# Local attention in front of two expert layers: filler products between half units taken out, weight loads and token preparation moved

## The chip, the cores and the metric

The kernel runs on one core of one Trainium2 chip. The metric is the device time of one execution in microseconds (us), as the median of several runs. A difference of less than about 0.2% can't be told from no change.

## The reference, cut to what matters

```python
# attention: batch 2, 8 heads, 768 positions, head_dim 64; chunks of 32 queries
for c in range(nc):
    k_full = concat([mem_k, k[l_start:r_end]])       # 8 memory keys, 16 left, 32 own, 8 right
    scores = scale * q_c @ k_full.T
    a = exp(scores - max(scores)); a = a / (sum(a) + 1e-9)
    out[chunk] = a @ v_full
x = out as 1536 tokens x 512
# layer 1: 4 experts (512 -> 1024 -> 512), summed with the tokens' probabilities p
for e in range(4):
    x1 += p[:, e] * (relu(x @ w1[e]) @ w2[e])
# layer 2: 512 -> 2048 -> 512, parametric relu
h = x1 @ w_in;  y = (max(h, 0) + alpha * min(h, 0)) @ w_out
```

## The kernel before

**Attention** is worked in 24 half units, numbered 0 to 23: a unit is 128 queries of one batch, a half unit four of its eight heads. The generator `half_unit` writes one out in five stages. `s`: 8 score products into a PSUM bank, then on VectorE (DVE) the row maximum `mx` and the subtraction into `pe_ring`. Then the exponential on ScalarE (ACT). `t`: four transposes of it on TensorE (PE) and their copy to `pt_ring` on ACT. `x`: 8 products with the values, then on DVE `dn`, `rd` and the normalised result `xs_t`. `xt`: two transposes of that and a copy to `acc` on ACT. After every fourth half unit a block of 128 token pairs is whole, and `prep_x` makes from it what the expert layers multiply: sums `st`, their rounded high part `xh` (casts on ACT) and the rest `xl`. For blocks 1, 2 and 5 (`FAST`) sums and rests are on DVE, for the others on POOL (GpSimd).

**The order of each engine** is fixed when the program is written out: a planner keeps a virtual clock `now`, to which each product adds a length (`T_S`, `T_X`, `T_T` for attention), and `att_poll` writes the next stage of a half unit once its latency (`LATE`, `LAT`) has passed on that clock. Up to four half units are live. Where no stage is due and nothing else may be written, `att_poll(force=True)` moves the clock on, and `fill` writes products of a zero tile `warm` (bank `wps`) for the time skipped, one per 0.11 us. 18 more stand at the very start.

**The expert layers** are products of 384 columns, in tiles of 384 token pairs: `gemm1` (banks a, b, c, d, then `g` and its high and low halves `gg`) and `gemm2` (banks `y`). The first tile needs blocks 0 to 2, the second blocks 3 to 5. So the program begins with attention alone, until half units 0 to 11 are done (here called **stretch A**); then comes `gemm1` of the first tile; then `gemm2` of the first tile, with the stages of the remaining half units written between its products; then, when those are used up, attention alone until half unit 23 is prepared; then `gemm1` of the second tile (from the first `gemm1` to here is **stretch B**). All that follows is products of the expert layers, with PE nearly full.

**Loads** are issued by the SP queue in program order. A half unit takes q (64x512 floats, 128 KB), k (64x672, 168 KB) and v (96x520, 195 KB). q and k have three buffers: those of half unit h+3 are issued after `s` of half unit h. Weights come as `raw` tiles of 512 KB (two for a pair of weight blocks) and are split into `wh` and `wl` by ACT and POOL. `gate` normalises the token probabilities on DVE, stores them (`p_dram`) and loads them back (`pb`), both on SP.

Of the kernel before, what the change touches and what calls it, by code (L numbers as in the profile page):

```python
# [30 lines left out]
NU = B * NBLK  # L31
# [36 lines left out]
def tile_kernel(ctx: ExitStack, tc: tile.TileContext, qk, mask, v, wa, wq, dpt, alpha, out):  # L68
    nc = tc.nc
    scale = 1.0 / float(D) ** 0.5  # L70
    pe_, dve, act, pool, sync = (Pinned(tc, e) for e in (nc.tensor, nc.vector, nc.scalar, nc.gpsimd, nc.sync))
# [7 lines left out]
    def bank(name):  # L79
        return ps.tile([P, 512], F32, tag="ps", name=name)  # L80
# [9 lines left out]
    nalpha = cp.tile([P, F2 // P], F32, name="nalpha")  # L90
# [4 lines left out]
    now = [0.0]  # L95

    def fill(n):

        if n > 0:
            wps = bank(f"wps{now[0]}")  # L100
            for _ in range(n):
                pe_.matmul(wps[:, :2 * P].rearrange("p (a n) -> p a n", n=P), warm, warm.unsqueeze(1).to_broadcast([P, 2, P]),
                           start=True, stop=True)
                now[0] += 0.11
# [5 lines left out]
    NI = NT // P  # L110
    p_dram = dp.tile([E, 2, NCOL], F32, name="p_dram")
    praw = cp.tile([P, E, NI], F32, name="praw")
# [82 lines left out]
    def load_v(hu):  # L195
        if hu >= 2 * NU:
            return
        u, half = divmod(hu, 2)
        dst = v_t[hu % RINGV // 2][:KEYS, hu % 2].rearrange("p w f -> p (w f)")
        sync.dma_start(dst, v[u, :, half])  # L200

    def half_unit(u, half):

        hu = 2 * u + half
        qv = q_t[hu % RING][:DQ].rearrange("p (h q) -> p h q", q=BLK)
        kv = k_t[hu % RING][:DQ].rearrange("p (h k) -> p h k", k=SPAN)
        vv = v_t[hu % RINGV // 2][:KEYS, hu % 2].rearrange("p w (h d) -> p w h d", d=D + 1)
        c, ab = divmod(u, 2)
        cols = slice(c * BLK, (c + 1) * BLK)
        hs = slice(2 * half, 2 * half + 2)  # L210
        nm = f"{u}_{half}"
        s_ps = bank(f"s{nm}")[:, :HH * KEYS].rearrange("p (h k) -> p h k", k=KEYS)
        for i in range(HH):
            for w in range(NW):
                r = slice(w * WIN, (w + 1) * WIN)
                mm(s_ps[r, i], qv[:, i, r], kv[:, i, w * STEP:w * STEP + KEYS], n=KEYS, took=T_S,
                   start=True, stop=True)
        load_half(hu + RING)
        mx = cp.tile([P, HH], F32, tag="mx", bufs=4, name=f"mx{nm}")
        dve.tensor_reduce(out=mx, in_=s_ps, axis=AX.X, op=ALU.max)  # L220
        pe = pe_ring[:, hu % 2]
        dve.tensor_tensor(
            out=pe, in0=s_ps, in1=mx.unsqueeze(2).to_broadcast([P, HH, KEYS]), op=ALU.subtract,
        )
        yield LATE
        act.activation(pe, pe, AF.Exp, scale=scale)
        yield LAT[0]
        t_ps = bank(f"t{nm}").rearrange("p (h q) -> p h q", q=BLK)
        for i in range(HH):
            pe_.transpose(t_ps[:KEYS, i], pe[:, i], ident)  # L230
            now[0] += T_T
        pt = pt_ring[:KEYS, hu % 2]
        act.copy(pt, t_ps[:KEYS])
        yield LAT[1]
        x_ps = bank(f"x{nm}")[:, :VW].rearrange("p (h d) -> p h d", d=D + 1)
        for i in range(HH):
            for w in range(NW):
                r = slice(w * WIN, (w + 1) * WIN)
                mm(x_ps[r, i], pt[:, i, r], vv[:, w, i], n=D + 1, took=T_X, start=True, stop=True)
        load_v(hu + RINGV)  # L240
        dn = cp.tile([P, HH, 1], F32, tag="dn", bufs=2, name=f"dn{nm}")
        dve.tensor_scalar_add(dn, x_ps[:, :, D:D + 1], 1e-9)
        rd = cp.tile([P, HH, 1], F32, tag="rd", bufs=2, name=f"rd{nm}")
        dve.reciprocal(rd, dn)
        xs = xs_t
        dve.tensor_tensor(out=xs, in0=x_ps[:, :, :D], in1=rd.to_broadcast([P, HH, D]), op=ALU.mult)
        yield LAT[2]
        xt_ps = bank(f"xt{nm}")[:, :2 * BLK].rearrange("p (c q) -> p c q", q=BLK)
        xf = xs.rearrange("p h d -> p (h d)")
        for z in range(2):  # L250
            pe_.transpose(xt_ps[:, z], xf[:, z * P:(z + 1) * P], ident)
            now[0] += T_T
        act.copy(acc[:, hs, ab, cols], xt_ps)
        if ab == 1 and half == 1:
            for _ in prep_x(c * BLK, BLK, c in FAST):
                yield 0.4

    att = {"next": 0, "start": 0.0, "done": 0, "over": set(), "live": [], "stage": [0] * (2 * NU + 1)}

    NEED = {0: 3, 2: 4}  # L260

# [6 lines left out]
    def att_poll(force=False):  # L268

        while True:  # L270
            due = [x for x in att["live"] if x[0] <= now[0] and clear(x[2])]
            room = att["next"] < 2 * NU and len(att["live"]) < LIVE and clear(att["next"])
            if due:
                x = due[0]
                try:
                    att["stage"][x[2]] += 1
                    lat = next(x[1])
                    x[0] = now[0] + lat
                except StopIteration:
                    att["live"].remove(x)  # L280
                    att["over"].add(x[2])
                    while att["done"] in att["over"]:
                        att["done"] += 1
            elif room and att["start"] <= now[0]:
                g = half_unit(*divmod(att["next"], 2))
                att["start"] = now[0] + (PACE0 if force else PACE)
                att["next"] += 1
                x = [0.0, g, att["next"] - 1]
                att["live"].append(x)
                x[0] = next(g) + now[0]  # L290
                att["stage"][x[2]] = 1
            elif force:
                times = [x[0] for x in att["live"] if clear(x[2])]
                if room:
                    times.append(att["start"])
                t = min(times)
                fill(int((t - now[0]) / 0.11))
                now[0] = max(now[0], t)
                continue
            else:  # L300
                return
            if force:
                return
# [6 lines left out]
    def load_raw(p, z):  # L310
        raw = bp.tile([P, 4, 256], F32, tag=f"raw{z}", name=f"raw{z}_{p}")
        src = wa[p] if p < NP1 else w2s[p - NP1]
        sync.dma_start(raw.rearrange("p a f -> p (a f)"), src[:, z * 1024:(z + 1) * 1024])
        raws[p, z] = raw
# [135 lines left out]
    pb_t = {}  # L450
# [186 lines left out]
    load_half(1)  # L637
    load_v(1)
    load_half(2)
    load_raw(0, 0)  # L640
    load_v(2)
    load_v(3)
    sync.dma_start(praw, dpt.rearrange("e (p i) -> p e i", i=NI))
    stream("w", weights())
    streams["w"][0] = PREP0
    acts = {}
    second = False
    for i, (what, k) in enumerate(order):
        p, c0, n = tiles[k]
        if what == 1:  # L650
            if p == 0:
                while att["done"] < 4 * -(-(c0 + n) // BLK):
                    att_poll(force=True)
                    prep_poll()
                    if att["next"] >= 4 and not second:
                        second = True
                        load_raw(0, 1)
                        nc.sync.dma_start(nalpha, alpha)
                    if att["done"] >= 4 and not pb_t:
                        gate()  # L660
                        dve.tensor_scalar_mul(nalpha, nalpha, -1.0)
                        load_pb(0, 0, FIRST[0][1])
            if k == k0:
                stream("c", convert())
                streams["c"][0] = now[0] + 20.0
            if k + 1 < len(tiles):
                p1, d0, m = tiles[k + 1]
                if p1 < NP1 and (2 * p1 * P // F1, d0, m) not in pb_t:
                    load_pb(2 * p1 * P // F1, d0, m)
            if p >= NP1 and f"x{c0}" in streams:  # L670
                prep_force(f"x{c0}", lambda: f"x{c0}" not in streams)
            hold[0] = p == 0
            acts[k] = gemm1(p, c0, n, k % 2 if p else 0, k == final[p])
        else:
            hold[0] = False
            change[0] = kx - 2 <= k <= kx + 1
            gemm2(p, c0, n, acts.pop(k), order[i - 1] == (1, k), k == final[p])
            if p == NP1 - 1:
                stream(f"x{c0}", transition(c0, n))
# [4 lines left out]

LAT = (1.0, 0.9, 1.3)
LATE = 1.5
T_S, T_X, T_T = 0.045, 0.036, 0.1
FAST = (1, 2, 5)
LIVE = 4
PACE = 2.3  # L690
PACE0 = 2.3
PREP0 = 6.0

DT = 1.1
DT_0 = 0.85
# [88 lines left out]
```

## Time and profile before

| | |
|---|---|
| median of 3 runs | 867.52 us (867.43 to 867.59) |
| profiled execution | 868.83 us, of it a span of 867.0 us |
| PE busy | 843.6 us (97%) |
| DVE busy | 607.1 us (70%) |
| POOL busy | 574.0 us (66%) |
| ACT busy | 336.4 us (39%) |
| first product of the first `gemm1` | at 62.62 us |
| first product of the second `gemm1` | at 106.62 us |

The span is what the trace covers; the profiled execution's own time is 1.83 us longer and lies 1.31 us above the median. A busy PE is not always useful: the filler products count as busy too, and matmuls overlap, so that two starts, not a duration, tell what one of them takes from the engine.

### The profile page before, as it was taken

To read this page: it belongs to the slowest core of one execution; us is meant where nothing else is said; L and a number is where in the kernel's file an instruction comes from. 1 tells how busy PE (TensorE), PEld (TensorE's weight loads), DVE (VectorE), ACT (ScalarE), POOL (GpSimd) and SP (SyncE) were. 2 spreads that over 40 slices of the span, in tenths; PEclk is the share of its full clock that TensorE was granted. 3 is DMA by queue.
4 is the path that set the end of the run, shared out by engine and by line. 5 is a ranking of instruction groups with operands and counts; after the bars stand their busy time and mean duration, and the time that the engine had idled before them with its cause. 6 is when DMAs were issued, how large, how long until landed. Compare 5 with 4: busy or idle time off the path is not lost.

```text
span 867.0 us, 14640 instructions
## 1 busy us (share of the span) xinstructions
PE 843.6 (97%) x5441; PEld 821.2 (95%) x5441; DVE 607.1 (70%) x1173; ACT 336.4 (39%) x738; POOL 574.0 (66%) x607
## 2 busy tenths in 40 slices
PE   7899999999999999999999999998799999999998
PEld 5788899999999999999999999997699999999998
DVE  2687676777767867678677677769867766776555
ACT  2465433323322323223232332324474645645442
POOL 2445447697766778669777697749567787774831
PEclk9999999999999999999999999999799999999999
DMA  9575211143122133212323213201011222121103
GB/s 186 150 192 140 60 49 49 38 128 116 37 85 85 63 113 107 63 60 87 108 68 104 85 37 103 72 9 50 24 49 62 86 86 97 54 70 37 62 1 146
DMA packets 28696, 69.76 MB, mean 80 GB/s; under 512 B 4664, under 2 KB 8888, under 8 KB 28624
## 3 DMA queue, kind: packets, MB, share of 16 engines
q1 hardware_dynamic: 28480, 68.76, 25.5%
q8 instruction: 43, 0.70, 0.3%
q14 instruction: 29, 0.24, 0.1%
q0 software_dynamic: 128, 0.04, 0.0%
q10 hardware_dynamic: 16, 0.02, 0.0%
HBM read 57.25 MB, written 11.56 MB: 79 GB/s over the span
## 4 chain that ended last, share of the span: by engine, by line
PE 88%; DVE 6%; ACT 2%; DMA 2%; POOL 1%; issue 1%; SPq 0%; DVEq 0%; POOLq 0%; ACTq 0%
PE y L62 45%; PE c L62 11%; PE a L62 11%; PE d L62 11%; PE b L62 5%; DVE st L62 2%; PE x L62 1%; PE s L62 1%; DVE xl L62 1%; PE t L62 1%; DMA k<-in_qk 1%; DVE g L62 1%; ACT xh L62 1%; DMA q<-in_qk 1%; DVE acc L62 1%
## 5 line engine op out<-in xcount | busy, mean ns | idle before, releaser
L62 PE MATMUL y<-gg,wh 128*128 128x384 f32 x1540 | 408.0, 341 | 8.4 <-POOL gg L62 4.8
L62 PEld LDWEIGHTS y<-gg,wh 128*128 128x128 f32 x1540 | 281.3, 190 | 11.7 <-POOL gg L62 6.4
L62 POOL TENSOR_TENSOR gg<-g,gg 128x384 fp32r<-128x384 f32 x192 | 198.6, 1043 | 107.7 <-ACT gg L62 96.2
L62 PE MATMUL y<-gg,wl 128*128 128x384 f32 (+1 forms) x770 | 260.8, 339 | 0.0
L62 DVE TENSOR_TENSOR acc<-y,acc 128x384 f32<-128x384 f32 x353 | 188.8, 551 | 67.3 <-PE y L62 66.1
L62 ACT CAST gg<-g 128x384 fp32r<-128x384 f32 x192 | 97.7, 511 | 169.8 <-DVE g L62 169.3
L62 POOL TENSOR_TENSOR wl<-raw,wh 128x256 fp32r<-128x256 f32 (+1 forms) x115 | 116.2, 1020 | 54.1 <-PE b L62 33.7
L62 PEld LDWEIGHTS y<-gg,wl 128*128 128x128 f32 x770 | 146.2, 190 | 0.2
L62 ACT COPY u<-a 128x384 f32<-128x384 f32 x48 | 23.0, 479 | 219.3 <-PE a L62 219.3
L62 POOL TENSOR_TENSOR wl<-s,wh 128x256 fp32r<-128x256 f32 x92 | 69.9, 767 | 16.4 <-ACT wh L62 16.2
L62 PE MATMUL c<-xh,wh 128*128 128x384 f32 x192 | 64.6, 336 | 2.0 <-DVE b L62 2.0
L62 PE MATMUL d<-xh,wh 128*128 128x384 f32 x192 | 64.4, 336 | 1.1 <-DVE t L62 1.1
L62 PE MATMUL a<-xh,wh 128*128 128x384 f32 x192 | 64.8, 338 | 0.3 <-ACT u L62 0.3
L62 PE MATMUL c<-xh,wl 128*128 128x384 f32 x192 | 64.5, 336 | 0.0
L62 PE MATMUL a<-xl,wh 128*128 128x384 f32 x192 | 64.4, 335 | 0.0
L62 PE MATMUL a<-xh,wl 128*128 128x384 f32 x192 | 64.3, 335 | 0.0
L62 PE MATMUL c<-xl,wh 128*128 128x384 f32 x192 | 64.3, 335 | 0.0
L62 PE MATMUL d<-xh,wl 128*128 128x384 f32 x192 | 64.2, 335 | 0.0
L62 PE MATMUL d<-xl,wh 128*128 128x384 f32 x192 | 64.2, 334 | 0.0
L62 DVE TENSOR_TENSOR u<-b,u 128x384 f32<-128x384 f32 x48 | 26.7, 557 | 51.4 <-PE b L62 46.9
L62 POOL TENSOR_TENSOR fl<-fl,fm 128x512 f32<-128x512 f32 x32 | 41.4, 1293 | 28.2 <-issue 19.0
L62 ACT CAST wh<-raw 128x256 fp32r<-128x256 f32 (+1 forms) x120 | 55.8, 488 | 0.9 <-PE a L62 0.6
(161 smaller groups left out, 1427.8 us busy)
## 6 DMA issues: line engine op xcount, KB each, us to landing
raw<-in_wa SPq DMA_DIRECT2D x32, 512.0 KB, 3.7
fr<-in_wq SPq DMA_DIRECT2D x32, 512.0 KB, 3.9
w2s<-fl SPq DMA_DIRECT2D x32, 256.0 KB, 2.3
raw<-w2s SPq DMA_DIRECT2D x16, 512.0 KB, 3.7
v<-in_v SPq DMA_DIRECT2D x24, 195.0 KB, 3.8
k<-in_qk SPq DMA_DIRECT2D x24, 168.0 KB, 3.5
q<-in_qk SPq DMA_DIRECT2D x24, 128.0 KB, 3.1
pb<-p_dram SPq DMA_DIRECT2D x8, 384.0 KB, 3.7
```

What stands on the lines that cost most here:

```text
L62: return self.tc.keep_in_program_order(f(*a, **kw))
```

## The change

The planner no longer writes filler products where it moves its clock on (the 18 at the start stay). Its lengths for attention's products are about doubled. The loads of the first weights, of the probabilities and of `alpha` are taken out of the head of the SP queue and are issued as later half units begin; `gate` waits for six half units done, not four; the preparation of weights starts at 12 on the planner's clock, not 6. `prep_x` of a block is not begun before the preparation of the block ahead of it is written out, and its steps on POOL are 1.0 apart, not 0.4.

```diff
         if ab == 1 and half == 1:
+            while att["x"] < c:
+                yield 0.2
             for _ in prep_x(c * BLK, BLK, c in FAST):
-                yield 0.4
+                yield 0.4 if c in FAST else 1.0
+            att["x"] = c + 1
...
-                t = min(times)
-                fill(int((t - now[0]) / 0.11))
-                now[0] = max(now[0], t)
+                now[0] = max(now[0], min(times))
...
     load_half(2)
-    load_raw(0, 0)
     load_v(2)
-    load_v(3)
-    sync.dma_start(praw, dpt.rearrange("e (p i) -> p e i", i=NI))
...
+    begun = [
+        (1, lambda: load_v(3)),
+        (1, lambda: load_raw(0, 0)),
+        (2, lambda: sync.dma_start(praw, dpt.rearrange("e (p i) -> p e i", i=NI))),
+        (6, lambda: sync.dma_start(nalpha, alpha)),
+        (7, lambda: load_raw(0, 1)),
+    ]
...
-                    if att["next"] >= 4 and not second:
-                        second = True
-                        load_raw(0, 1)
-                        nc.sync.dma_start(nalpha, alpha)
-                    if att["done"] >= 4 and not pb_t:
+                    while begun and att["next"] >= begun[0][0]:
+                        begun.pop(0)[1]()
+                    if att["done"] >= 6 and not pb_t:
...
-T_S, T_X, T_T = 0.045, 0.036, 0.1
+T_S, T_X, T_T = 0.095, 0.075, 0.105
-PREP0 = 6.0
+PREP0 = 12.0
```

The order on PE early in stretch A; a name such as `s1_0` is the bank of unit 1, half 0, which is half unit 2. Before:

```order
L62 MATMUL x0_0_200<-v0_110,pt_ring_113 64x65 x8
L62 LDWEIGHTS warm_74
L62 MATMUL wps4.447999999999997_215<-warm_74 128x256
L62 MATMUL s1_0_217<-k2_109,q2_106 64x96 x8
L62 LDWEIGHTS warm_74
L62 MATMUL wps4.959999999999999_231<-warm_74 128x256
L62 MATMUL t0_1_233<-ident_69,pe_ring_112 96x128 x4
L62 LDWEIGHTS warm_74
L62 MATMUL wps5.559999999999998_239<-warm_74 128x256
L62 MATMUL xt0_0_241<-ident_69,xs_t_114 128x128 x2
```

The same place in the changed program:

```order
L62 MATMUL x0_0_171<-v0_110,pt_ring_113 64x65 x8
L62 MATMUL s1_0_186<-k2_109,q2_106 64x96 x8
L62 MATMUL t0_1_200<-ident_69,pe_ring_112 96x128 x4
L62 MATMUL xt0_0_206<-ident_69,xs_t_114 128x128 x2
L62 MATMUL x0_1_210<-v0_110,pt_ring_113 64x65 x8
```

The stages follow each other in the same order and the `warm` products are gone. In the whole program 185 of them go, 133 in stretch A and 52 at the end of stretch B.

The order on SP, after the loads of the first two half units (`q2` is the third of the three buffers). Before:

```order
L62 DMA q2_106<-in_qk 64x512
L658 DMA nalpha_79<-in_alpha 128x16
L62 DMA k2_109<-in_qk 64x672
L62 DMA raw0_0_130<-in_wa 128x1024
L62 DMA v1_111<-in_v 96x520 x2
L62 DMA praw_100<-in_dpt 128x4x12
L62 DMA q0_104<-in_qk 64x512
L62 DMA k0_107<-in_qk 64x672
```

The same place in the changed program:

```order
L62 DMA q2_106<-in_qk 64x512
L62 DMA k2_109<-in_qk 64x672
L62 DMA v1_111<-in_v 96x520
L62 DMA q0_104<-in_qk 64x512
L62 DMA k0_107<-in_qk 64x672
L62 DMA v1_111<-in_v 96x520
L62 DMA raw0_0_146<-in_wa 128x1024
```

The 512 KB of weights, the `alpha` load and `praw` now stand behind q and k of half unit 3.

The order on ACT where block 0 is prepared: `xh<-st0` are the two casts that need POOL's sums, the `ACTIVATE` is an exponential, `pt_ring<-t3_1` the copy of half unit 7's transposes. Before:

```order
L62 CAST wh1_0_4_440<-s_0_265 128x256
L62 CAST xh_101<-st0_410 128x4x128
L62 COPY pt_ring_113<-t2_1_463 96x512
L62 COPY acc_103<-xt2_0_475 128x2x128
L62 CAST wh1_0_3_499<-s_0_265 128x256
L62 CAST xh_101<-st0_410 128x4x128
L62 ACTIVATE pe_ring_112<-pe_ring_112 128x384
```

The same work in the changed program:

```order
L62 CAST wh1_0_4_411<-s_0_287 128x256
L62 CAST xh_101<-st0_353 128x4x128
L62 COPY acc_103<-xt2_1_430 128x2x128
L62 CAST wh1_0_3_452<-s_0_287 128x256
L62 ACTIVATE pe_ring_112<-pe_ring_112 128x384
L62 COPY acc_103<-xt3_0_471 128x2x128
L62 CAST xh_101<-st0_353 128x4x128
L62 COPY pt_ring_113<-t3_1_476 96x512
```

The second cast stood ahead of half unit 6's exponential and one half unit behind the first; it now stands ahead of half unit 7's copy. From the first product of the second `gemm1` on, every engine has the same instructions in the same order in both programs.

## Rows read from the trace of the kernel before

**Rows 1.** Windows by stretch: length, busy us (instructions) by engine, clock, DMA share, GB/s.

```profile
0.00:62.62 62.62, 54.87 (x714) 43.38 (x714) 35.47 (x89) 27.87 (x63) 25.57 (x35) 0.95 0.75 177
62.62:70.80 8.18, 7.89 (x45) 7.27 (x43) 7.96 (x19) 2.94 (x7) 1.29 (x2) 1.00 0.61 169
70.80:97.20 26.40, 26.40 (x354) 22.16 (x352) 19.55 (x51) 15.11 (x34) 15.34 (x17) 1.00 0.38 104
97.20:106.62 9.42, 8.67 (x100) 7.48 (x99) 4.52 (x13) 4.36 (x10) 3.71 (x5) 1.00 0.19 60
```

**Rows 2.** Timeline of PE, first scores and half unit 3: start, length, idle before and releaser.

```profile
5.60 0.88 PE L62 MATMUL s<-k,q 68*64 68x96 f32 x16 [0.71 <-DMA k<-in_qk]
...
17.60 0.94 PE L62 MATMUL s<-k,q 68*64 68x96 f32 x16 [2.88 <-DMA k<-in_qk]
```

**Rows 3.** Window from the first loads to that wait's end.

```profile
2.00:17.60 15.60, 11.93 (x139) 9.15 (x136) 4.88 (x12) 3.66 (x8) 4.60 (x9) 1.00 1.04 210
```

**Rows 4.** Groups by form, 0 to 106.62 us: weight loads of all filler products.

```profile
L62 PEld LDWEIGHTS <-warm 128*128 128x128 bf16 x203 | 20.1, 105 | 6.3 <-DVE tiny L88 1.0 <-issue 0.2
```

**Rows 5.** Timeline of PE, one half unit's period in stretch A.

```profile
52.12 0.83 PE L62 MATMUL s<-k,q 68*64 68x96 f32 x16
52.88 0.64 PE L62 MATMUL t<-ident,pe_ring 128*96 128x128 f32 x4
53.36 0.60 PE L62 MATMUL ps28.832000000000058_828<-warm 128*128 128x256 bf16 x4
53.80 0.38 PE L62 MATMUL xt<-ident,xs_t 128*128 128x128 f32 x2
...
54.33 0.69 PE L62 MATMUL x<-v,pt_ring 96*64 96x65 f32 x16
...
55.27 0.88 PE L62 MATMUL s<-k,q 68*64 68x96 f32 x16
```

**Rows 6.** Timeline of DVE, the same period.

```profile
53.09 0.55 DVE L62 TENSOR_REDUCE mx<-s 128x4 f32<-128x384 f32 x1
53.74 0.56 DVE L62 TENSOR_TENSOR pe_ring<-s,mx 128x384 f32<-128x384 f32 x1
55.06 0.16 DVE L62 TENSOR_SCALAR dn<-x 128x4 f32<-128x4 f32 x1 [0.77 <-PE x L62]
...
55.47 0.42 DVE L62 TENSOR_TENSOR xs_t<-x,rd 128x256 f32<-128x256 f32 x1
```

**Rows 7.** Timeline of ACT, the same period.

```profile
53.62 0.58 ACT L62 COPY pt_ring<-t 96x512 f32<-96x512 f32 x1 [1.40 <-PE t L62]
...
54.49 0.53 ACT L62 ACTIVATE pe_ring<-pe_ring 128x384 f32<-128x384 f32 x1
```

**Rows 8.** Timeline of ACT, the second cast of block 0.

```profile
34.37 0.62 ACT L62 CAST xh<-st 128x512 fp32r<-128x512 f32 x1 [3.03 <-POOL st L62]
```

**Rows 9.** Windows, DVE alone: block 1's preparation (tile st); gate and alpha.

```profile
43.90:51.60 7.70, 3.71 (x6) 1.00 0.87 185
...
33.70:37.10 3.40, 3.17 (x8) 0.74 0.34 91
```

**Rows 10.** Timeline of PE, after that cast.

```profile
35.46 1.09 PE L62 MATMUL t<-ident,pe_ring 128*96 128x128 f32 x4 [2.43 <-ACT pe_ring L62]
...
37.97 1.03 PE L62 MATMUL x<-v,pt_ring 96*64 96x65 f32 x16
```

**Rows 11.** Windows as in rows 1, there and in the second layer's start.

```profile
35.00:40.00 5.00, 4.54 (x47) 3.73 (x48) 2.87 (x7) 1.97 (x5) 2.68 (x3) 0.66 0.13 29
606.00:612.00 6.00, 3.21 (x16) 2.25 (x15) 5.93 (x10) 4.76 (x10) 4.25 (x4) 1.00 0.00 0
612.00:614.00 2.00, 2.00 (x9) 2.00 (x8) 0.65 (x2) 1.29 (x3) 0.73 (x1) 0.55 0.00 0
```

**Rows 12.** Timeline of PE, end of stretch B: last transposes, first product of the second gemm1.

```profile
103.86 0.38 PE L62 MATMUL xt<-ident,xs_t 128*128 128x128 f32 x2
...
106.62 0.42 PE L62 MATMUL a<-xh,wh 128*128 128x384 f32 x1
```

More of the change, by code (lines that the diff above doesn't have):

```diff
@@ L254, in half_unit @@
         if ab == 1 and half == 1:
+            while att["x"] < c:
+                yield 0.2
             for _ in prep_x(c * BLK, BLK, c in FAST):
-                yield 0.4
-    att = {"next": 0, "start": 0.0, "done": 0, "over": set(), "live": [], "stage": [0] * (2 * NU + 1)}
+                yield 0.4 if c in FAST else 1.0
+            att["x"] = c + 1
+    att = {"next": 0, "start": 0.0, "done": 0, "over": set(), "live": [], "x": 0, "stage": [0] * (2 * NU + 1)}
     NEED = {0: 3, 2: 4}
@@ L646, in tile_kernel @@
     acts = {}
-    second = False
+    begun = [
[5 more added lines that the diff above has]
+    ]
     for i, (what, k) in enumerate(order):
```

## The prediction, written before the changed kernel ran

> **What bounds the kernel now.** I read the page first: PE is 97% busy, so only places where its work is not the expert layers' own, or where it waits, can give time. The window table by stretch shows where those are [rows 1]: stretch A, 62.62 us in which not one expert product runs; the first `gemm1`, 8.18 us; the interleaved part of stretch B, 26.40 us with PE busy throughout; and its end, 9.42 us of attention alone. In the busy time of A and of B's end the reader must see two things mixed, attention and filler. From 106.62 us on both programs have the same order on all engines, so I take the remaining 760 us as unchanged, and the prediction is when the second `gemm1` starts.
>
> How much the fillers weigh is read from the groups: 203 weight loads of `warm`, 18 of them at the very start, so 185 between half units [rows 4], 133 in A and 52 in B's end. One period of A in PE's timeline shows what one takes [rows 5]: scores start at 52.12, transposes at 52.88, four fillers run from 53.36 to 53.80 (0.11 us each), `xt` at 53.80, and the next scores start at 55.27. The period is 3.15 us; attention's own part is 0.76 (s) + 0.48 (t) + 0.22 (xt) + 0.62 (x) = 2.08 us, the rest is eight fillers and their gaps. So 185 fillers are 20 us of PE, but they are gained only if nothing else was being waited for beneath them. What else each half unit needs is on DVE [rows 6]: maximum and subtraction 53.09 to 54.30, 1.2 us, and `dn`, `rd`, `xs_t` 55.06 to 55.89, 0.83 us, so 2.03 us, nearly as much as PE's 2.08.
>
> **Stretch A, to half unit 6: the loads.** Half unit 3 waited for its k, 2.88 us, until 17.60 [rows 2], while the DMA share was 1.04 at 210 GB/s [rows 3]: that part was bound by loads, with 512 KB of weights ahead of that k. Now they stand behind it. To the k of half unit 6 the new list has 7 x 296 KB of q and k, 6 x 195 KB of v, 512 + 24 KB of others: 3778 KB, 3869 thousand bytes, 18.4 us at 210 GB/s. With the 2 us before the first bytes [rows 3] that is 20.4 us. But loads in flight share the rate: in before, half unit 3 needed 2568 thousand bytes in 15.6 us, 165 GB/s, by which it would be 25.4. I take 22 us, nearer to the fast end because less is in flight at once.
>
> **Half units 6 to 9: PE and one cast.** From s of 6 to s of 9 PE has 3 s, 3 t, 4 x, 4 xt: 2.28 + 1.44 + 2.48 + 0.88 = 7.1 us. Waits which fillers covered appear: from the end of t the copy takes until x may start (t ends near 53.4, copy 53.62 to 54.20 [rows 7], so 0.75 us), and where only `xt` stands between, 0.5 us is left, twice; an exponential may add 0.4 (scores end, then 1.2 us of DVE and 0.53 of ACT [rows 6, 7]). Sum 8.5. The second cast of block 0 waited 3.03 us for POOL's sums and ACT's queue waited with it [rows 8]; PE stood 2.43 us for it [rows 10]. In the new order it stands ahead of half unit 7's copy, and POOL's chain (eight operations after the block is whole) is as long as before while PE gets there sooner. Bounds: nothing, if the steps now 1.0 apart are slow enough, and 3.0 as before. I take 2.0, since the new order moves it back by one position only. So s of 9 starts at 22 + 8.5 + 2.0 = 32.5.
>
> **Half unit 9 to the first product: DVE.** From here DVE has more to do than PE: maximum and subtraction of 9 to 14, 6 x 1.2 = 7.2; `dn` to `xs_t` of 8 to 13, 6 x 0.83 = 5.0; gate and `alpha`, which filled 3.3 us of DVE [rows 9]; block 1's preparation, 3.7 [rows 9]; and four of six operations of block 2's, 2.2. Sum 21.4 us, from 33.4 (0.9 after the start of those scores) to 54.8; then `xt` of 13 and `x` of 14, 0.84. First product at 55.6 us in place of 62.62: **7.0 us** earlier. Gate also holds the SP queue (store, load back), so q and k of half units 13 and 14 come late; DVE is that far behind already, which hides it; without that cover I would price it as the one wait for a load in before, 2.88 us [rows 2].
>
> **The clock.** After PE stood 2.43 us the five microseconds from 35.00 have a mean clock of 0.66, that is 3.4 us at 1.2 GHz [rows 11], and t took 1.09 us there against 0.64, x 1.03 against 0.69 [rows 10, 5]. A fall does not need one long wait: from 606 to 612 PE was busy 3.21 of 6 us at full clock, and in the next two the mean was 0.55 [rows 11]. Without fillers A looks like that. The Trainium skill, "TensorE: Matmul & The Clock Gate", section "A second HAM failure mode: psum-queue depth-cycling", says that frequent short idle times between groups of matmuls make the clock swing between its two levels, and that throughput falls by the re-warming; rows 11 agree, and by it A would be the slow case below, 864 us. In my sum A costs nothing more, because the loads and then DVE set its pace and hide PE's doubled lengths; for the tail see next.
>
> **Stretch B.** `gemm1` 8.18 us as before: DVE was busy 7.96 of it, with the same work now. After it 8 s, 9 t, 9 x and 10 xt are left to do (in before 8, 10, 10 and 11), and the new order sets all but the last `xt` among the 48 y products or right behind them, where the old 26.40 us held 8 of each and left two t, two x and three xt to the bare end: 26.40 + 0.48 + 0.62 + 0.22, less gaps, 27.6. Then the bare end of half unit 23: 0.55 (copy before x), 1.05 (`dn` to `xs_t`, 0.83 and its start [rows 6]), and from the last `xt` to `gemm1` 106.62 - 103.86 = 2.76 [rows 12], a chain through ACT and POOL that fillers only accompanied. Sum 8.18 + 27.6 + 4.36 = 40.1 us against 44.0: **3.9 us**. PE stands for most of the last 4 us, so I expect `gemm1` to begin at 1.2 GHz; a spell of 3.4 us loses half of itself at most, 1.7; taken **1.5 us**, since in before this stretch was warm.
>
> **Sum.** 7.0 + 3.9 - 1.5 = 9.4 us. Against the execution's own 868.83 us that is 859.4; the median stands 1.3 us lower, so 858.1, rounded to **858 us**. The loads' upper bound (25.4) and the cast's (3.0) would add 4.4, the lower bounds take 3.6 off.
>
> **Rivals.**
> *Slow clock through A.* Without `warm` products PE drops to 1.2 GHz and stays there until `gemm1`. For: rows 11. Against: the loads and DVE have the pace anyway, and a PE that is twice as slow is also busier. Price: s about 1.4 (twice 0.76 less start cost, estimate), t 0.87, x 0.93, xt 0.4, so 3.6 us; 15 half units from 5.60 give 59.6. With `gemm1` begun cold (1.7) and B as above: gain 3.0 - 1.7 + 2.4 = 3.7, 864 us.
> *Slower than before.* The same, and the wait from t to x (0.55) is never covered: 4.15 us for each half unit, first product at 67.9, start of the second `gemm1` at 67.9 + 1.7 + 40.1 + 1.5 = 111.2, 4.6 us late: 872 us. It decides from 3.85 us for each half unit on (63.3 us for the first product, where B's gain is used up). Against: before's own period with fillers is 3.15, and its wait from t to x lay mostly beside the next s.
> *Loads alone.* If DVE's work packs into the load-bound part and the cast doesn't block, only the loads are left: 9093 KB to half unit 15's k and v of 14, 9311 thousand bytes, 44.3 us + 2 + the last products, first product at 48: gain 14.6 + 3.9 - 1.5 = 17.0, 850.5 us. Against: 35.47 us of DVE in A [rows 1] cannot begin before the first scores (6.5) and its gate and preparation come late in order.
> *No effect.* Every filler stood where something was awaited, so the waits stay: 866 to 869 us. Against: DVE 35.47 and PE's own 2.08 a period are both far below A's 62.62 us [rows 1].
>
> **Chances.** Forecast (853 to 861) 0.52; slow clock 0.20; loads alone (under 853) 0.15; no effect 0.05; slower 0.08. A measurement here can tell about 0.2%, 1.7 us. Faster by more: the forecast, loads alone, and most of the slow clock (0.17), 0.84; within: 0.03 of that and no effect, 0.08; slower 0.08. The range leaves one in ten out on each side: below, half of loads alone, 850; above, the slower case and a little of no effect, 866.
>
> **What would show it.** Half unit 3's scores start near 13 us with little wait for k; s of 6 near 22, of 9 near 32.5; DVE nearly gapless from there to the first `a` at 55 to 56 (a later one with PE's clock at 0.5 throughout is the slow clock; a DVE with gaps and a DMA share near 1 is loads alone); the second `gemm1` 9 to 11 us sooner than 106.62, its first 3 us at half clock; and from then on the old times, shifted. Wrong if the shift changes after the second `gemm1`, or if ACT's queue stands longer than 3 us behind the cast.

## The result: slower by 1.07%, and the profile after

The changed kernel takes 876.99 us (median of 4 executions, 876.87 to 877.41) beside 867.56 us of the kernel before: a ratio of 1.0107 [1.009, 1.0125]. The prediction had 858 us and a range that ended at 866, so it was wrong in sign, and the time lies above the range. The profiled execution took 877.41 us with a span of 875.6, 8.6 us more than before. Two slow executions among those of the experiments (1031.24 and 2113.6 us) are left out of all medians and ratios below.

On the page of after two lines of the 40 slices (21.9 us each) already show the place:

```profile
PE   8999989999999999999999999998699999999998
...
PEclk7557989999999999999999999999799999999999
```

PE is as busy in the first slices as anywhere, but its clock there is 0.7, 0.5, 0.5, 0.7. The windows of after, columns as in [rows 1], first by stretch and then more finely:

```profile
0.00:70.43 70.43, 64.96 (x602) 50.05 (x602) 37.27 (x95) 30.34 (x67) 24.46 (x35) 0.57 0.68 160
70.43:79.73 9.30, 9.30 (x45) 9.27 (x43) 7.05 (x16) 2.01 (x5) 1.71 (x2) 0.78 0.50 147
79.73:111.80 32.07, 28.87 (x378) 23.79 (x376) 22.31 (x60) 18.00 (x41) 17.76 (x19) 1.00 0.35 89
...
7.00:9.50 2.50, 1.46 (x20) 1.11 (x20) 1.29 (x3) 0.52 (x1) 0.00 (x0) 1.00 1.03 195
9.50:10.00 0.50, 0.00 (x0) 0.00 (x0) 0.47 (x2) 0.48 (x1) 0.00 (x0) 0.74 1.19 240
...
12.00:40.00 28.00, 26.96 (x254) 20.97 (x252) 12.47 (x33) 12.40 (x29) 12.10 (x15) 0.50 0.74 175
40.00:70.43 30.43, 29.24 (x276) 22.29 (x273) 21.86 (x54) 14.82 (x34) 9.46 (x11) 0.50 0.55 141
...
51.88:70.43 18.55, 18.54 (x171) 13.78 (x170) 11.68 (x27) 9.54 (x21) 4.85 (x5) 0.50 0.59 152
...
70.43:74.40 3.97, 3.97 (x14) 3.97 (x13) 2.25 (x5) 0.78 (x2) 0.70 (x1) 0.50 0.65 181
...
75.00:79.00 4.00, 4.00 (x25) 4.00 (x24) 3.82 (x9) 1.23 (x3) 1.01 (x1) 1.00 0.40 141
```

Stretch A ends at 70.43, not at 62.62 as in [rows 1] and not at the predicted 55.6. PE was busy 56.2 of the 58.4 us from 12.00 to 70.43 (96%), all of it at a clock of 0.50, the lower level of 1.2 GHz; DVE was busy 34.3 of them and the DMA share was 0.74 and 0.55. So PE had become the bound of A. From 51.88 on it didn't stand at all (18.54 of 18.55 us), and the clock stayed at 0.50 even so. PE's timeline of after shows where the clock fell, one period of A, and where the clock rose again (start, length, idle before and releaser):

```profile
8.03 0.88 PE L62 MATMUL s<-k,q 68*64 68x96 f32 x16 [1.45 <-DMA k<-in_qk]
8.84 0.64 PE L62 MATMUL t<-ident,pe_ring 128*96 128x128 f32 x4
10.15 1.14 PE L62 MATMUL x<-v,pt_ring 96*64 96x65 f32 x16 [0.67 <-ACT pt_ring L62]
...
51.88 1.55 PE L62 MATMUL s<-k,q 68*64 68x96 f32 x16
53.36 0.69 PE L62 MATMUL xt<-ident,xs_t 128*128 128x128 f32 x2
53.98 1.14 PE L62 MATMUL x<-v,pt_ring 96*64 96x65 f32 x16
55.05 1.09 PE L62 MATMUL t<-ident,pe_ring 128*96 128x128 f32 x4
56.07 1.55 PE L62 MATMUL s<-k,q 68*64 68x96 f32 x16
...
70.43 0.69 PE L62 MATMUL a<-xh,wh 128*128 128x384 f32 x1
...
74.12 0.53 PE L62 MATMUL b<-xh,wl 128*128 128x384 f32 x1
74.44 0.42 PE L62 MATMUL d<-xh,wh 128*128 128x384 f32 x1
74.69 0.34 PE L62 MATMUL d<-xl,wh 128*128 128x384 f32 x1
...
110.41 0.41 PE L62 MATMUL xt<-ident,xs_t 128*128 128x128 f32 x2 [1.03 <-DVE xs_t L62]
111.80 0.44 PE L62 MATMUL a<-xh,wh 128*128 128x384 f32 x1 [0.98 <-ACT xh L62]
113.20 0.69 PE L62 MATMUL a<-xl,wh 128*128 128x384 f32 x1 [0.96 <-POOL xl L62]
...
118.49 0.52 PE L62 MATMUL d<-xh,wl 128*128 128x384 f32 x1
118.81 0.42 PE L62 MATMUL a<-xh,wh 128*128 128x384 f32 x1
```

PE stood 1.45 us for a k and then 0.67 us for a copy, and the clock fell within the second of these waits (0.74 from 9.50 to 10.00, by which the fall is near 9.75); from then on x takes 1.14 us and s 1.55, beside 0.69 and 0.83 in [rows 5]. The period is read from start to start: from 51.88 to 56.07 it is 1.48 (s) + 0.62 (xt) + 1.07 (x) + 1.02 (t), together 4.19 us, with no wait in it. With eight fillers it was 3.15 [rows 5]. The k of half unit 3 is no longer waited for; that s starts at 15.18 instead of 17.60. The clock rises 4.0 us after the first expert product: the products stand 0.32 us apart until 74.44 and 0.17 to 0.18 from 74.69 on.

The account of the 8.6 us, from the starts of the two `gemm1`: stretch A +7.81 (70.43 against 62.62); the first `gemm1` +1.12 (9.30 against 8.18, begun at half clock); from there to the second -3.75 (32.07 against 35.82); and from its first product to the end of the span +3.42 (763.80 against 760.38). The last comes from the bare end: the second product waits for the rest `xl` until 113.20, and nearly all up to 118.81 stand 0.32 us apart. The 19th product starts 7.01 us after the first; in the kernel before, whose order is the same here, 3.23 us after its first, at 106.62 [rows 12]:

```profile
109.85 0.33 PE L62 MATMUL a<-xh,wh 128*128 128x384 f32 x1
```

### The profile page after: what moved, and what is told of

The parts are those of the page before. It is cut to its first block, busy times and chain, and to the rows that moved or that the text cites. A ratio compares the mean times of both kernels' runs of the same rounds, so it can differ in the third digit from the quotient of the medians.

```text
span 875.6 us, 14271 instructions
## 1 busy us (share of the span) xinstructions
PE 851.8 (97%) x5256; PEld 826.5 (94%) x5256; DVE 607.8 (69%) x1173; ACT 337.3 (39%) x738; POOL 573.5 (65%) x607
## 4 chain that ended last, share of the span: by engine, by line
PE 91%; DVE 5%; ACT 1%; issue 1%; DMA 1%; POOL 0%; SPq 0%; DVEq 0%; ACTq 0%
PE y L62 45%; PE a L62 11%; PE d L62 11%; PE c L62 11%; PE b L62 6%; PE s L62 3%; PE x L62 2%; PE t L62 2%; DVE st L62 2%; PE xt L62 1%; DVE xl L62 1%; DVE g L62 1%; DMA k<-in_qk 1%; DVE acc L62 1%; ACT xh L62 0%
```

## Experiments

Theory (**clock**): without fillers PE drops to 1.2 GHz in A, attention alone doesn't bring it back, and PE's doubled lengths set A's pace. Rival (**plan**): the moved loads, held preparation and new lengths make A longer, whatever the clock. Ratios are to the kernel before on the same chip, whose medians there were 866.4 to 867.0 us, with single executions from 863 to 873. With such a spread the intervals are up to 0.5% on either side, wider than the 0.2% that the prediction took as the least that can be told.

### Fillers and plan apart

*The new plan with its fillers:* the line that was removed stands again, with the new lengths (86 fillers in A, 45 at B's end).

```diff
-                now[0] = max(now[0], min(times))
+                t = min(times)
+                fill(int((t - now[0]) / 0.11))
+                now[0] = max(now[0], t)
```

> The changed program with its filler products back (the planner's clock, and so the order of everything else, stays as in the changed program; 86 fillers in stretch A, 45 at the end of stretch B). Theory clock: attention's own products do not hold PE at 2.4 GHz and the fillers do; then the loads and VectorE set A's pace as in the prediction, the first product comes near 55.6 us, the second gemm1 near 96 us, the median near 857 us. Rival order: the new order of loads and preparation is itself what costs; then the time stays at 872 to 877 us although the clock is full. Rival PE: in A fillers are on the path one for one, and the time goes back to 867.

*The old plan without fillers:* the kernel before with only the reverse of that edit.

> The kernel before with only its 185 fillers between half units taken out; the order of all else is as before. Theory clock: PE falls to 1.2 GHz near 10 us and stays there until the first gemm1, about 4.1 us for each half unit, first product at 68 to 71 us, median 874 to 879 us. Rival order: the loss comes from the moved loads and the held preparation, which are not here; then 855 to 867 us.

*Fillers at the end of B alone:* as the first, with `if att["done"] >= 12:` ahead of the `fill`.

> The changed program with fillers back only in forced waits after half unit 12, that is at the end of stretch B (45). Theory clock: A stays at 1.2 GHz (first product near 70 us as in the changed program); the second gemm1 begins at 2.4 GHz and gains the half of 5 us that it ran slow, so 873 to 875 us. Rival: the end of B waits for ACT and POOL alone and the fillers are worth nothing, 877 us.

Measured: 868.37 us, ratio 1.0032 [0.9996, 1.0067], for the new plan with fillers; 876.67, 1.0115 [1.0069, 1.0161], for the old plan without; 875.81, 1.0103 [1.0049, 1.0158], with fillers at B's end alone. So taking fillers out costs 1.15% (10 us) in the old plan and 1.0107 against 1.0032, or 0.75% (6.5 us), in the new, which the intervals don't tell apart; and the plan as a whole gains nothing with or without them. Of the forecasts the clock theory's for the old plan (874 to 879) was met; its 857 for the new plan with fillers was not, and that time lies nearest to the rival that puts the fillers on the path (867). The windows further down show what the theory had left out. PE's timeline of the old plan without fillers:

```profile
17.35 1.55 PE L62 MATMUL s<-k,q 68*64 68x96 f32 x16 [2.52 <-DMA k<-in_qk]
...
21.57 1.50 PE L62 MATMUL s<-k,q 68*64 68x96 f32 x16
...
25.73 1.49 PE L62 MATMUL s<-k,q 68*64 68x96 f32 x16
...
70.14 0.69 PE L62 MATMUL a<-xh,wh 128*128 128x384 f32 x1
```

The wait for k is the old one; the period of 4.16 us (a wait of 0.30 us ahead of x is part of it here) and the first product at 70.14 are close to those of after. The loads, moved or not, have no part in it. With fillers at B's end alone the first product comes at 71.21, cold; the second `gemm1` starts at full speed but at 114.58, 2.8 us later than in after. Its 19th product comes at 117.83 and not at 118.81: 1.0 us of the gain is left, less than the medians can tell. A window of that run and PE's timeline in the next:

```profile
20.00:40.00 20.00, 19.37 (x180) 14.59 (x176) 9.31 (x25) 9.08 (x21) 8.51 (x11) 1.00 0.54 152
```

```profile
48.75 1.54 PE L62 MATMUL s<-k,q 68*64 68x96 f32 x16
50.09 1.08 PE L62 MATMUL x<-v,pt_ring 96*64 96x65 f32 x16
```

The clock column reads 1.00 there and also from 40 to 70, but s takes 1.54 us, as at half clock in after. The other executions of this kernel show mean clocks of 0.955 at nearly the same spans (872.8 to 875.2 against 874.0), so the record of this one execution is wrong and the lengths decide.

In the new plan with its fillers the clock moves both ways:

```profile
15.00:20.00 5.00, 3.06 (x47) 2.39 (x44) 2.31 (x6) 2.28 (x5) 2.81 (x4) 1.00 1.07 207
20.00:25.00 5.00, 4.35 (x54) 3.52 (x56) 1.79 (x5) 1.38 (x3) 0.73 (x1) 0.74 0.69 151
25.00:30.00 5.00, 5.00 (x49) 3.71 (x47) 1.88 (x5) 2.64 (x7) 1.51 (x3) 0.58 0.76 217
30.00:40.00 10.00, 9.24 (x153) 7.53 (x151) 6.25 (x18) 6.37 (x16) 8.40 (x10) 1.00 0.55 158
40.00:45.00 5.00, 2.35 (x23) 1.54 (x19) 4.69 (x13) 2.51 (x7) 2.42 (x4) 0.79 0.15 34
45.00:50.00 5.00, 5.00 (x49) 3.85 (x49) 3.77 (x9) 2.20 (x6) 0.48 (x2) 0.53 0.86 220
50.00:60.00 10.00, 9.34 (x145) 7.22 (x140) 7.04 (x18) 6.30 (x15) 2.97 (x4) 1.00 0.94 213
```

```profile
36.96 0.83 PE L62 MATMUL s<-k,q 68*64 68x96 f32 x16
...
44.06 0.66 PE L62 MATMUL xt<-ident,xs_t 128*128 128x128 f32 x2 [2.50 <-DVE xs_t L62]
...
62.78 0.41 PE L62 MATMUL xt<-ident,xs_t 128*128 128x128 f32 x2 [1.42 <-DVE xs_t L62]
...
64.03 0.69 PE L62 MATMUL a<-xh,wh 128*128 128x384 f32 x1
```

The two falls shown here come after slices in which PE waited (busy 3.06 of 5 us, and 2.35 of 5), and each time the clock came back within A, which it never did in after. By the clock of these windows the two spells are 13.6 us at the lower level, an estimate of at most 6.8 us of lost work; the first product comes 8.4 us later than the forecast's 55.6. So fillers between the half units don't hold the clock through every wait. The long wait is no longer for a cast on ACT but for `xs_t`, which on DVE stands behind `gate` (39.06 to 42.31) and two sums of block 1.

### How many fillers

*One filler at most for each skip* (41 in all), *three at most* (96), and *half more* (206), each an edit of the `fill` line of the new plan:

```diff
+                fill(min(1, int((t - now[0]) / 0.11)))
...
+                fill(min(3, int((t - now[0]) / 0.11)))
...
+                t = max(now[0], t)
+                fill(int(1.5 * (t - now[0]) / 0.11))
+                now[0] = t
```

> The changed program with at most one filler in each forced wait (41 in all in place of 131). Theory clock, few are enough: the clock stays full in A and the time is near that of the program with all fillers, within 2 us. Theory clock, few are not enough: the clock falls near 10 us as in the changed program and the time is 874 to 879 us.

> The changed program with at most three fillers in each forced wait (96 of its 131). Theory clock: with more filler the fall comes later or is made good sooner than with one in each wait, so 867 to 871, between the program with all (868) and the one with at most one (871, runs from 866 to 876). Rival: any limit is as bad as none, 875 to 877.

> The changed program's order with one and a half times the fillers that its own forced waits give (206 in place of 131). Theory clock: the three falls of the clock in stretch A (near 22, 44 and 62 us) become fewer and the time is 862 to 866 although PE has 8 us more filler. Rival PE: the fillers are on the path and the time is 870 to 876.

Measured: 871.06 (865.67 to 875.85), ratio 1.0046 [1.0011, 1.0082]; 869.20 (864.34 to 872.17), 1.0029 [1.0004, 1.0055]; 871.72 (864.82 to 874.84), 1.005 [1.0023, 1.0077]. With at most one, single executions lie anywhere between after and the kernel before, and the profiled one (875.85) was cold, from 20 to 60 us at 0.50. The three differ from each other and from the full number by less than their intervals tell: few fillers recover part of the time in many executions, and more of them gain nothing further. The time with half more is the one that the rival with fillers on the path gave (870 to 876). Its profiled execution shows both sides: one fall of the clock in A fewer and the first product at 62.06 instead of 64.03, but 29 more fillers behind it and the second `gemm1` at 108.26 instead of 106.77.

*One burst:* after, with 40 fillers in a row when half unit 8 begins and none besides the first 18.

```diff
+                    if att["next"] == 8 and not burst:
+                        burst.append(now[0])
+                        fill(40)
+                        now[0] = burst[0]
```

> The changed program (no fillers in waits) with one burst of 40 fillers before half unit 8, long enough to bring the clock back. Theory clock (attention's products alone do not hold the higher level): it falls again within a few us, the burst costs its 6 us and the time is 878 to 884. Rival (the clock falls only at the early waits for loads and attention would hold it once it is up): the rest of A runs at 2.4 to 3.2 us for each half unit, 866 to 872.

Measured: 882.44 us, 1.0179 [1.0159, 1.0199]. Windows of it, and PE's timeline behind the burst (35.32 to 41.26):

```profile
35.00:38.00 3.00, 3.00 (x19) 2.03 (x16) 1.12 (x2) 0.35 (x1) 2.92 (x4) 0.50 0.31 92
38.00:40.00 2.00, 2.00 (x18) 1.66 (x17) 0.00 (x0) 0.00 (x0) 0.13 (x1) 0.86 0.04 13
40.00:44.00 4.00, 3.64 (x54) 3.06 (x51) 1.52 (x5) 1.37 (x4) 0.72 (x1) 1.00 0.14 46
44.00:46.00 2.00, 0.98 (x20) 0.85 (x20) 0.27 (x1) 1.83 (x5) 1.30 (x2) 0.85 0.61 164
46.00:60.00 14.00, 12.82 (x126) 10.08 (x124) 11.25 (x30) 6.83 (x16) 5.25 (x6) 0.50 0.56 137
```

```profile
43.29 0.41 PE L62 MATMUL xt<-ident,xs_t 128*128 128x128 f32 x2 [0.36 <-DVE xs_t L62]
...
45.16 0.98 PE L62 MATMUL x<-v,pt_ring 96*64 96x65 f32 x16 [1.02 <-ACT pt_ring L62]
```

The burst brings the clock up; attention alone keeps it up for some four microseconds, it falls behind the waits of 0.36 and 1.02 us, and PE stays at half clock to the first expert product at 76.04. That agrees with the clock theory, and the time is as it forecast (878 to 884): it is not enough that the clock is raised once. Fillers between the half units also stand where PE would wait, and the burst has none there.

### The parts of the plan, with fillers

*Loads alone:* in the kernel before, the loads of the first weights, `praw` and `alpha` are moved as in the change (the second weights and `alpha` at half unit 4, not at 6 and 7); `gate`, the lengths and the fillers stay.

```diff
-    load_raw(0, 0)
...
-    load_v(3)
-    sync.dma_start(praw, dpt.rearrange("e (p i) -> p e i", i=NI))
...
+        (1, lambda: load_v(3)),
+        (1, lambda: load_raw(0, 0)),
+        (2, lambda: sync.dma_start(praw, dpt.rearrange("e (p i) -> p e i", i=NI))),
+        (4, lambda: load_raw(0, 1)),
+        (4, lambda: sync.dma_start(nalpha, alpha)),
```

> The kernel before with its fillers and its planner's lengths; only the loads of the first weights, the probabilities and alpha move behind q and k of half unit 3 as in the change. Theory of the prediction's first term (the loads bound the start): half unit 3's scores start near 13 us in place of 17.6 without the fall of the clock behind that wait, the first product comes 3 to 5 us sooner, median 862.5 to 865. Rival: the wait goes to later half units (k of 4 and 5, as in the changed plan with fillers, 1.2 and 1.4 us), and the time stays within 1.5 us of before.

*Held preparation alone:* the kernel before with only this.

```diff
+            while att["x"] < c:
+                yield 0.2
...
-                yield 0.4
+                yield 0.4 if c in FAST else 1.0
+            att["x"] = c + 1
```

> The kernel before with its fillers and lengths; only the preparation of token blocks is held as in the change (one block after another, steps on POOL 1.0 apart). Theory: the cast of block 0 no longer stands ahead of its sums in ACT's queue, the wait of 2.43 us near 33 us and the slow spell behind it go, median 863 to 866. Rival: the gate on VectorE (3.3 us) stands in the same place and takes over the wait; no change within 1.5 us.

*Both of them:*

> The two moves together on the kernel before, fillers and planner's lengths kept. If both terms of the prediction are real they add: 859 to 862. If each wait is replaced by another: 866 to 868. Beats both kernels if anything of the change does.

*The whole new plan with fillers but the old lengths:* `T_S, T_X, T_T = 0.045, 0.036, 0.1`.

> The changed program with its fillers back and the planner's three lengths as they were (185 fillers in place of 131); loads, hold, gate at six and weights at 12 as in the change. Theory (the longer lengths cost, because they leave fewer fillers and more waits in which the clock falls): like the two moves on old lengths, 861 to 864. Rival (gate at six done or the later weights cost): 867 to 869, like the new plan with its fillers.

Measured:

| kernel | median us | ratio |
|---|---|---|
| loads alone | 866.53 | 0.9988 [0.9966, 1.001] |
| held preparation alone | 861.73 | 0.9946 [0.9923, 0.9968] |
| both | 862.66 | 0.9954 [0.9931, 0.9977] |
| new plan, fillers, old lengths | 862.80 | 0.995 [0.9928, 0.9973] |
| new plan, fillers, new lengths | 868.37 | 1.0032 [0.9996, 1.0067] |

The held preparation gains 0.54%, the loads nothing that can be told, nor do the later `gate` and weights (the fourth row against the third), and the new lengths lose 0.8%, more than the preparation gains. The number of fillers in A isn't how the lengths do that: with half more of them (132 in A, where the kernel before has 133) the first product still comes at 62.06, beside 56.76 with the old lengths and 133. Single executions mislead here: the profiled one of the loads alone, 861.88 us and nearly the fastest of twelve, has its first product at 56.74, and the median shows no gain. Held preparation alone, windows and PE's timeline:

```profile
35.00:40.00 5.00, 3.22 (x48) 2.47 (x47) 4.66 (x14) 3.59 (x8) 3.09 (x4) 1.00 0.30 71
40.00:45.00 5.00, 5.00 (x50) 4.03 (x48) 4.83 (x11) 2.41 (x6) 0.72 (x1) 0.66 0.89 216
```

```profile
39.73 0.44 PE L62 MATMUL xt<-ident,xs_t 128*128 128x128 f32 x2 [1.71 <-DVE xs_t L62]
...
56.84 0.42 PE L62 MATMUL a<-xh,wh 128*128 128x384 f32 x1
```

The 2.43 us wait for the cast [rows 10] is gone and the clock of 35 to 40 is 1.00, not 0.66 [rows 11]; the next wait, 1.71 us for `xs_t` behind `gate` (35.27 to 36.65 on DVE) and two sums of block 1 (to 38.93), stands there instead and the fall follows it. The first product is at 56.84, the second `gemm1` at 99.27.

*That wait too:* held preparation, and `gate`'s steps written out one for each forced poll instead of all at once; then the same with the moved loads; then each of the two kernels without the loads again, on one chip.

```diff
     def gate():
+        yield
...
-                        gate()
-                        dve.tensor_scalar_mul(nalpha, nalpha, -1.0)
-                        load_pb(0, 0, FIRST[0][1])
+                        next(gates, None)
```

> The kernel before with the held preparation, and the gate's operations written one at a time between half unit stages in place of all at once. Theory (behind the hold the gate is the next wait: 1.71 us of PE for VectorE and a slow spell behind it): 858 to 860.5, 1.5 to 3 us better than the hold alone. Rival: VectorE has no room left there and the wait only moves: 861 to 863.

> The kernel before with its fillers and lengths, the held preparation, the spread gate and the moved loads together. Theory (the wait of half unit 3 for its k is real, 0.5 to 4.2 us in the profiles so far, and the moved loads take it away): 2 to 4 us better than hold and spread gate without them, 857 to 860. Rival (the loads are bound by the rate, and the wait goes to later half units): the same as those within 1.5 us, 861 to 863.

> Hold and spread gate once more, on the same chip as the run with moved loads and the run with the hold alone. Theory (spreading is worth something where the loads don't wait): 1 to 2 us better than the hold alone. Rival: the same within 1 us, 861 to 863.

> The hold alone once more, as the measure for the other two: 860 to 863 if its gain of 5 us holds on another chip.

Measured: spread gate 862.16, 0.9944 [0.9927, 0.9961], and again 861.78, 0.9953 [0.9931, 0.9975]; with the loads 861.10, 0.9943 [0.9923, 0.9963]; held preparation alone again 861.14, 0.9936 [0.9919, 0.9953]. Neither the gate nor the loads add anything that can be told; all four times are those that the rivals gave (861 to 863), or for the hold alone the expected one. Held preparation in the kernel before, fillers kept, is as good as any and the smallest edit; it beats both kernels.

## Why the prediction was wrong

**The failing step: the clock.** The text said "In my sum A costs nothing more, because the loads and then DVE set its pace and hide PE's doubled lengths". They don't. PE's own part of a period was at hand, 2.08 us at full clock [rows 5]; doubled it is 4.16, and 15 of them after 5.60 end at 68.0, later than in the kernel before. The loads to half unit 15, by the working of the rival "Loads alone", end near 46, and DVE was busy only 35.47 us in all of A [rows 1]. Nothing there could hide 62 us of PE. Measured were 4.19 us for a half unit and 70.43 us to the first product; DVE's sum from half unit 9 on was about right (21.4; busy 21.86 from 40.00 on), but PE took 30.43 us over that stretch and set the pace.

**The rivals.** "Slower than before" had the place, the slow clock, and almost the size: 4.15 us for each half unit, first product 67.9, 872 us, deciding from 3.85 on. It had 8 in 100. That its period came out so close was partly luck: it is 3.6 us of products and a wait of 0.55 us from t to x, and the period measured in after is 4.19 us of products without a wait. "Slow clock through A" has the same 3.6, by lengths of single groups; from start to start s takes 1.48 and not 1.4, x 1.07 and not 0.93, t 1.02 and not 0.87, xt 0.62 and not 0.4. The first `gemm1`, begun cold, cost 1.12 us more (1.7 in the rivals' sums, nothing in the forecast's).

**Swing or stay.** In after the clock fell once, near 9.75 us, and stayed at the lower level until 74.4; in the new plan with fillers it fell and rose again within A. The Trainium skill, "TensorE: Matmul & The Clock Gate", section "A second HAM failure mode: psum-queue depth-cycling", has it swing between its two levels where PE often stands for a short time. The run with fillers agrees; after differs from it, its cost being that of one long stay. The Trainium skill's section "Seeing it yourself" on that page warns that the clock events of a trace have been seen to be unreliable; the run with fillers at B's end alone agrees, with 1.00 beside an s of 1.54 us.

**Stretch A, the other terms.** Moving the loads did take the wait for the k of half unit 3 away (s at 15.18 against 17.60), but in the new plan with fillers, where that s starts at 13.34 as forecast, the next two wait for theirs (1.21 and 1.38 us); moved alone the loads are worth nothing that can be told. s of half unit 6 and of 9 were forecast at 22 and 32.5; in the new plan with fillers they start at 23.90 and 36.96, with a cold spell between, and with the old lengths at 23.77 and 33.11. "DVE nearly gapless" from there did not come about either: DVE was busy 21.86 of 30.43 us from 40.00 on in after. The first product at 55.6 is close to what A does with the whole plan, fillers and old lengths (56.76), and with fillers and held preparation alone (56.84); so the size of the term at full clock was nearly right, in part by luck since the waits in it are others, but it needs the fillers that the change removes, and the new lengths take it away (64.03).

**The cast.** It was charged 2.0 us as a wait that stays. With fillers and the held preparation it goes, and a wait for `xs_t` behind `gate` and the sums of block 1 (1.70 to 2.50 us) takes its place; the cost of `gate` had been put in DVE's sum and not seen as a wait that PE stands in.

**Stretch B.** Interleaved part and bare end: -3.75 us, forecast -3.9. The sum is right by two misses that cancel: the last `xt` starts 30.7 us after the first `gemm1` ends (110.41 less 79.73) and not 29.2, and the second `gemm1` 1.39 us after it, not 2.76. The chain of 2.76 is there, but it ends at the second product (113.20), which waits for `xl`. The cold start was foreseen in kind, priced 1.5, and cost 3.42 with that wait: 17 steps from the second product to the 19th, nearly all 0.32 us and not 0.17, are 2.6 of it, the wait 1.1, and 0.4 is made good later. The times after that are only shifted.

**Open.** How the new lengths cost 0.8% with fillers in place; why spreading `gate`, which cuts its wait to 0.51 us, moves the median nowhere; and whether attention's own products could hold the higher clock if nothing waited: every kernel without fillers had a wait early in A. That they don't raise it is shown (18.54 of 18.55 us busy at 0.50).

## What to carry to other kernels

Before taking out products that keep an engine busy, add up the useful ones at half clock, start to start, over the whole stretch, and compare that sum with the loads and with the other engines; only if it is still below one of them does the lower clock cost nothing. A change made of several parts is worth splitting before it is judged: here one part gained 0.5%, one lost more than that, one did nothing, and the fourth cost 1%.

## What the runs showed of the hardware that was not expected

- PE stayed at 1.2 GHz for 64 us (9.75 to 74.4) while it was busy 96% of the time with attention's products, and rose 4.0 us after the first expert product; 40 fillers in a row raised it about 3 us after they began, and it fell again some four microseconds after the last of them.
- One execution's record has the clock at 1.00 where products took their half-clock lengths (s 1.54 us, 0.83 at full clock).
- The wait for the k of half unit 3, with the loads in the same order, was 2.88 us [rows 2], 2.52 in the old plan without fillers, 1.29 in one execution with held preparation, 4.22 in one with the gate spread, and in another with held preparation that s starts at 14.62 after 0.50 us that the trace puts down to no load. Single executions of the kernel before differ by up to 10 us on the chips of the experiments; that this wait is the reason is not shown.
